# A fourth output buffer and a re-ordered step list in a fused chunk attention and leaky-ReLU MLP kernel

## Chip, cores and metric

The kernel runs on one core of a Trainium2 chip. The metric is the device time of one execution in microseconds (us), the median of several executions. TensorE appears in the profile as PE, its weight load as PEld, VectorE as DVE, ScalarE as ACT, GpSimd as POOL, and SyncE, which here only issues DMAs, as SP. The profile's times of day are counted from the start of the profiled span.

## What is computed

Attention is cut into chunks of 64 rows that attend only to themselves; its result is the input of a two-layer network with a leaky ReLU.

```python
B, H, S, D = 8, 8, 576, 64            # q, k, v: float32
scores = scale * matmul(q_c, k_c.T)   # per chunk of 64 rows
attn = exp(scores - max) / (sum + 1e-9)
x = (attn @ v_c) -> [4608, 512]       # heads side by side
h = x @ w_in                          # [512, 2048]
g = maximum(0.01 * h, h)
out = g @ w_out                       # [2048, 512], float32
```

## The kernel before

**Tiling.** The 4608 tokens are 36 attention units `u` of 128 tokens (two chunks, eight heads), and 19 network blocks `j`: two of 128 tokens and 17 of 256. Each block has one or two output tiles `(j, t)` of 128 tokens by 512 float32.

**The steps.** The whole program is a string, `ORDER` (L588 on); each word calls one small function, and the words are recorded one after the other. Every engine then runs its own instructions strictly in that order and waits by semaphores. The words that matter here, for a unit `u`:

- `g` loads q and k (DMAs issued by POOL, which also converts to 16 bits); `tdq`, `tdk` transpose them with DMAs issued by SP (early units use TensorE, `tq`, `tk`, and copies `q`, `k`); `cq` copies the transposed q into a padded tile `QZ`.
- `s` makes the scores on PE, `m`, `b`, `x` the maximum, subtraction and exponential, `z` the sum and its reciprocal, `n` the normalisation (a mark `'` behind the word puts it on POOL). `e` and `c` transpose it by PE and a copy, or `d` by a DMA of SP. `v` multiplies by v on PE, and `a` writes the result into `xT`.

For a block `j`: `M` and `G` are the first layer and its leaky ReLU in the plain form (blocks 0 to 4, 16 matmuls of 128 columns for each `M`). From block 5 on the first layer uses seven half-size products, `V` (eight matmuls of 128 columns), with input sums `xs`, and `ls`, `lf`, `la`, `lp` around them. The second layer of blocks 2 to 18 has seven products `R` (eight matmuls of 256 columns), with sums `sum` of the hidden tile and `comb`, which combines the products in PSUM banks into output tiles. `WS` and `W` make weight sums; `vl`, `L`, `Q`, `P` load v and the weights. `y` writes zeros. The mark `'` selects the other engine: ACT or DVE for copies, DVE or POOL for sums.

**Output tiles.** `st j.t` stores an output tile by a DMA that SP issues. Tiles of blocks 0 to 3 live in six buffers shared with another tile (`xkeep`); those of later blocks in three buffers (`osb`, L547). Which buffer of a pool a tile gets, and which of the eight PSUM banks, is read from a second string, `BANKS` (L60), one digit for each tile. The first `comb` that writes a tile has to wait until the store of the buffer's tile before has landed in DRAM. By the digits the three buffers hold, one after the other, tiles (4,1), (6,1), (7,0), (9,1) and on; (4,0), (5,1), (6,0), (8,0) and on; (5,0), (7,1), (8,1), (10,1) and on.

SP issues its DMAs one after the other: a store that stands behind a transposing DMA waits until that one's input is there. POOL likewise issues loads in turn with its own arithmetic.

Of the kernel before, what the change touches and what calls it, by code (L numbers as in the profile page):

```python
# [8 lines left out]
FP16 = mybir.dt.float16  # L9
# [7 lines left out]
def kernel(  # L17
# [32 lines left out]
    HELD = 4  # L50
# [5 lines left out]
    sbp = ctx.enter_context(tc.tile_pool(name="k_sb", bufs=1))  # L56
# [4 lines left out]
        "00011221230456070010314000500217016214111507112302062123352232304113201152167534233330222053401467100010334400"  # L61
        "13571420161745522311176641100130110257726203232163050000260305117211223311412623372234204331530060152344200551"
        "76234101020110541013101230220213272225140377333432006115001323040400114216105400241310267220022231311010114501"
        "20302011321141031325600202117010123032141013321723602700020334320410006101054120230105571104231101013212132223"
        "11173512271210632123416056144001202011322463002000602002110201273560300103311240120017011526411233342211712117"
        "30211760251213310314042330004123214003205600510031047223010526023052302110743112107213311343122116401101300371"
        "22420013213340503301105101017033102066146250311531210022127022413100002013471121702210311033430310711425330260"
        "02301257120457301061523222240310060004020113112353002142162111121340200111312701002032304353102213154002144303"
        "0106411732452411010211460174025322315100132310744021021127110405"
# [87 lines left out]
    warm = sbp.tile([128, 384], FP16, name="warm")  # L157
# [387 lines left out]
    def output(j, t):  # L545
        if (j, t) not in ob:
            tag, bufs = ("xkeep", 6) if j < HELD else ("osb", 3)  # L547
            ob[j, t] = sb([128, d_model], FP32, "ob", tag, bufs)
        return ob[j, t]
# [32 lines left out]
    def store(j, t, c=2):  # L582
# [146 lines left out]
```

## Time and profile before

| what | us |
|---|---|
| median of 3 timed runs (lowest, highest) | 277.01 (276.88, 281.54) |
| the profiled execution | 278.08 |
| its span, first to last instruction | 276.3 |
| PE busy | 264.6 |
| DVE, ACT, POOL busy | 236.6, 185.4, 142.9 |

The table of stretches that the prediction shows gives, for each piece of the span, how long each engine was busy; what is missing to the length of the stretch on PE is idle time of PE. A timeline row gives the start, the duration, the engine, the line and the operation with its tiles (out<-in), and in brackets the idle time of that engine before it and what ended it. Rows of equal instructions are merged (x8 are eight of them). In a chain-of-waits row "DMA out_dram<-ob" the first number is when SP issued the store, the second how long it was until it had landed.

### The profile page before, as it was taken

Reading aid. Unit: us, or ns where it says so; the run is one execution under the profiler, and the core shown is the slowest. Engines: PE = TensorE matmul, PEld = TensorE weight load, DVE = VectorE, ACT = ScalarE, POOL = GpSimd, SP = SyncE. Lnnn points to the kernel's source line nnn. Section 1 sums busy time; section 2 is a strip of 40 time slices with the busy share of each in tenths; the row PEclk is TensorE's granted clock in tenths of the full one; section 3 lists DMA queues with packets and bytes.
Section 4 is the critical chain, followed back from the end, with each engine's and each line's share of the span. In section 5 each row is a group of like instructions: output and inputs, shape, how many; then the busy total and the mean of one; then the engine's idle time right before and its main releaser. Section 6 shows DMA issues by size and latency. Waiting matters only on the chain.

```text
span 276.3 us, 9429 instructions
## 1 busy us (share of the span) xinstructions
PE 264.6 (96%) x3909; PEld 243.5 (88%) x3909; DVE 236.6 (86%) x487; ACT 185.4 (67%) x380; POOL 142.9 (52%) x174
## 2 busy tenths in 40 slices
PE   7889999999999998999899999999999999999994
PEld 4579967998999997889799999999999999999993
DVE  7785699988799997798799999998898996888873
ACT  4675735897859996679567784977878655536330
POOL 8858556887557949378549249646333122000000
PEclk9999999999999999999999999999999999999998
DMA  9999999999899999999999999999999231420323
GB/s 146 158 189 193 207 174 155 155 93 149 95 158 153 137 130 168 179 184 124 177 184 166 138 165 122 201 200 176 149 162 122 78 40 49 30 78 2 116 77 115
DMA packets 157611, 37.97 MB, mean 137 GB/s; under 512 B 148608, under 2 KB 153088, under 8 KB 157568
## 3 DMA queue, kind: packets, MB, share of 16 engines
q0 software_dynamic: 111392, 18.10, 98.8%
q1 hardware_dynamic: 45136, 19.02, 41.9%
q8 instruction: 30, 0.49, 0.8%
q10 hardware_dynamic: 1040, 0.26, 0.4%
q14 instruction: 13, 0.11, 0.1%
HBM read 36.70 MB, written 9.44 MB: 167 GB/s over the span
## 4 chain that ended last, share of the span: by engine, by line
PE 70%; DVE 12%; DMA 8%; ACT 5%; issue 2%; POOL 2%; SPq 0%; DVEq 0%; ACTq 0%; POOLq 0%
PE prX L525 16%; PE xbank L442 13%; PE prZ L525 9%; DMA out_dram<-ob 8%; PE hT L370 7%; PE xz L442 7%; PE prW L525 4%; PE seed L442 4%; PE oP L571 2%; PE xp L335 2%; PE Sp L277 2%; DVE SG L502 2%; DVE z L299 2%; DVE mx L284 2%; ACT gT L384 2%
## 5 line engine op out<-in xcount | busy, mean ns | idle before, releaser
L525 PEld LDWEIGHTS <-SG 128*128 128x128 f16 x544 | 51.1, 98 | 7.6 <-issue 2.1
L442 PEld LDWEIGHTS <-WS 128*128 128x128 f16 x896 | 54.6, 98 | 0.9
L309 POOL TENSOR_TENSOR en<-ex,z 128x512 f16<-128x512 f16 x30 | 31.5, 1056 | 40.1 <-DVE z L305 32.3
L442 PEld LDWEIGHTS <-w_inT 128*128 128x128 f16 x672 | 41.2, 98 | 1.6 <-issue 1.0
L525 PEld LDWEIGHTS <-gT 128*128 128x128 f16 x400 | 37.5, 98 | 3.9
L117 POOL DMA_DIRECT2D q_in<-in_q_dram x39 | 33.6, 867 | 14.1 <-DMA QT<-q_in 9.9
L117 POOL DMA_DIRECT2D k_in<-in_k_dram x39 | 32.8, 845 | 5.2 <-DMA VB<-in_v_dram 1.7
L525 PE MATMUL prX<-TW,SG 128*128 128x256 f16 x272 | 35.1, 273 | 0.0
L442 PE MATMUL xbank<-xs,WS 128*128 128x128 f16 x448 | 33.1, 219 | 0.0
L370 PE MATMUL hT<-xT,w_inT 128*128 128x128 f16 x512 | 31.7, 219 | 1.4 <-ACT ex L294 0.9
L370 PEld LDWEIGHTS <-w_inT 128*128 128x128 f16 x512 | 29.4, 98 | 1.9 <-issue 1.7
L299 DVE TENSOR_REDUCE z<-ex 128x8 f32<-128x512 f16 x36 | 24.0, 674 | 4.7 <-ACT ex L294 4.4
L200 ACT ACTIVATE keep<-prX 128x256 f32<-128x256 f32 x42 | 16.0, 382 | 16.8 <-PE prX L525 14.6
L284 DVE TENSOR_REDUCE mx<-Sp 128x8 f32<-128x512 f32 x36 | 24.3, 677 | 1.5 <-PE Sp L277 1.4
L502 DVE TENSOR_TENSOR SG<-gT 128x1024 f16<-128x1024 f16 x34 | 23.9, 707 | 2.0 <-ACT gT L384 1.7
L122 POOL DMA_DIRECT2D VB<-in_v_dram x24 | 23.3, 981 | 3.1 <-DMA w_outT<-in_moe_w_out_dram 3.1
L461 DVE TENSOR_TENSOR xz<-xbank,x 128x512 f32<-128x512 f32 x28 | 19.0, 690 | 3.3 <-PE xbank L442 1.6
L384 ACT ACTIVATE gT<-xz 128x512 f16<-128x512 f32 x28 | 16.6, 594 | 6.6 <-PE xz L442 6.5
L200 ACT ACTIVATE xT<-xp 128x512 f16<-128x512 f32 x26 | 15.4, 593 | 8.0 <-PE xp L335 7.8
L461 DVE TENSOR_TENSOR x<-xbank,x 128x512 f32<-128x512 f32 x28 | 19.0, 682 | 2.0 <-PE xbank L442 1.9
L384 ACT ACTIVATE gT<-seed 128x512 f16<-128x512 f32 x28 | 16.6, 598 | 6.1 <-PE seed L442 4.9
L384 ACT ACTIVATE gT<-xbank 128x512 f16<-128x512 f32 x28 | 16.1, 595 | 5.8 <-PE xbank L442 5.3
(97 smaller groups left out, 576.5 us busy)
## 6 DMA issues: line engine op xcount, KB each, us to landing
out_dram<-ob SPq DMA_DIRECT2D x35, 256.0 KB, 3.9
q_in<-in_q_dram POOLq DMA_DIRECT2D x31, 128.0 KB, 6.6
k_in<-in_k_dram POOLq DMA_DIRECT2D x31, 128.0 KB, 6.8
VB<-in_v_dram POOLq DMA_DIRECT2D x8, 288.0 KB, 7.9
VB<-in_v_dram POOLq DMA_DIRECT2D x16, 144.0 KB, 7.7
w_inT<-in_moe_w_in_dram POOLq DMA_DIRECT2D x8, 256.0 KB, 7.4
w_outT<-in_moe_w_out_dram POOLq DMA_DIRECT2D x4, 512.0 KB, 11.5
q_in<-in_q_dram POOLq DMA_DIRECT2D x8, 64.0 KB, 8.0
```

The lines of the kernel that those rows point to most:

```text
L117: nc.gpsimd.dma_start(out=to, in_=rows)
L122: nc.gpsimd.dma_start(out=VB[b % NVB][m * CH:(m + 1) * CH, h0:h1, :, m * CH:(m + 1) * CH].rearrange("p h c d -> p (h c) d"), in_=v[b, m * ...
L200: nc.scalar.activation(out=to, in_=of, func=AFT.Copy, bias=0.0, scale=1.0)
L284: nc.vector.tensor_reduce(out=MX[u], in_=SP[u], axis=AXL.X, op=ALU.max)
L299: nc.vector.tensor_reduce(out=Z[u, 0], in_=EX[u], axis=AXL.X, op=ALU.add)
L309: (nc.gpsimd if other else nc.vector).tensor_tensor(out=EN[u], in0=EX[u], in1=Z[u, 2].unsqueeze(2).to_broadcast((128, 8, CH)), op=ALU.mult)
L370: nc.tensor.matmul(out=hT[:, i, :], lhsT=w_inT[:, t, fc * 128:(fc + 1) * 128], rhs=xT[:, t, r0:r0 + tb], start=(i == 0 and t == 0), stop=( ...
L384: nc.scalar.activation(out=to, in_=of, func=AFT.Prelu, bias=0.0, scale=1.0, alpha=0.01)
L442: nc.tensor.matmul(out=to[:, i, :], lhsT=left[:, t, i * 128:(i + 1) * 128], rhs=right[:, t], start=(n in (1, 5) and t == 0 and i == 0), st ...
L461: nc.vector.tensor_tensor(out=to, in0=XB[j, s], in1=X5[j, s], op=ALU.add)
L502: (nc.gpsimd if other else nc.vector).tensor_tensor(out=SG[j, n], in0=x, in1=y, op=op)
L525: nc.tensor.matmul(out=to, lhsT=left[:, f, :], rhs=right[:, f, :], start=(f == 0 and (n in (1, 2, 5) or where == "Z3")), stop=(f == HF - 1 ...
```

## The change

Four edits. The pool `osb` has four buffers. The constant tile `warm`, which the first idle matmuls read, gets the memory of one of them (its tag). `BANKS` and `ORDER` are written anew from the 114th word on: the same 1551 words, in another order, and 134 of them with the mark `'` set or taken away.

```diff
@@ BANKS @@
-        "00011221230456070010314000500217016214111507112302062123352232304113201152167534233330222053401467100010334400"
+        "00011221230456070010314000500217016214111507112302062123352232304113201152167435233330204220335215416000300133"
...
-    warm = sbp.tile([128, 384], FP16, name="warm")
+    warm = sbp.tile([128, 384], FP16, name="warm", tag="osb4_0")
...
-            tag, bufs = ("xkeep", 6) if j < HELD else ("osb", 3)
+            tag, bufs = ("xkeep", 6) if j < HELD else ("osb", 4)
...
@@ ORDER @@
-        "P1 M0.2.0 z3.1 P2 z3.2 n3 G2.1.1 g7 M1.2.0 e3 M2.2.1 c3' v3 k4 a3 s4 M2.0.2 M2.1.2 M2.2.2 m4 b4 WS1.0 x4 z4.0 "
+        "P1 M0.2.0 z3.1 P2 z3.2 n3 M2.2.1 G0.2.0 G2.1.1 e3 M1.2.0 g6 k4 c3' G2.2.1 y5 s4 v3 M0.3.0 a3 G0.3.0 m4 M2.0.2 "
```

The four buffers now hold (4,0), (6,0), (8,1), (10,0) and on; (4,1), (6,1), (8,0), (10,1) and on; (5,0), (7,1), (9,0) and on; (5,1), (7,0), (9,1) and on. Of the words whose mark changes, the net effect is that six `a`, six `cq` and five `lp` go from DVE to ACT, seven `comb` from ACT to DVE, and five `xs` from DVE to POOL; `lf`, `ls`, `n`, `y` and `z` change by one each.

Three places where the order differs. First the queue of SP from the store of tile (4,0) on (`out_0_dram<-ob_1922`, and after the change `ob_1839`). Before it reads:

```order
L264 DMA_TRANSPOSE QT_2376<-q_in_1830 128x4x128
L326 DMA_TRANSPOSE et_2399<-en_2397 128x4x128
L585 DMA out_0_dram<-ob_1922 128x512
L258 DMA_TRANSPOSE KT_2411<-k_in_1832 128x4x128
L264 DMA_TRANSPOSE QT_2431<-q_in_2268 128x4x128
L326 DMA_TRANSPOSE et_2443<-en_2429 128x4x128
L258 DMA_TRANSPOSE KT_2476<-k_in_2270 128x4x128
L264 DMA_TRANSPOSE QT_2514<-q_in_2317 128x4x128
L258 DMA_TRANSPOSE KT_2642<-k_in_2319 128x4x128
L585 DMA out_0_dram<-ob_2422 128x512
```

The next store there, `ob_2422`, is tile (5,1), which uses the buffer of `ob_1922`. After the change the same stretch of SP is:

```order
L585 DMA out_0_dram<-ob_1839 128x512
L258 DMA_TRANSPOSE KT_2136<-k_in_1692 128x4x128
L585 DMA out_0_dram<-ob_2044 128x512
L585 DMA out_0_dram<-ob_1546 128x512
L264 DMA_TRANSPOSE QT_2242<-q_in_2006 128x4x128
L264 DMA_TRANSPOSE QT_2266<-q_in_2178 128x4x128
L326 DMA_TRANSPOSE et_2312<-en_2225 128x4x128
L258 DMA_TRANSPOSE KT_2314<-k_in_2008 128x4x128
L326 DMA_TRANSPOSE et_2358<-en_2346 128x4x128
L585 DMA out_0_dram<-ob_2397 128x512
```

Tiles (4,0) and (4,1), `ob_1839` and `ob_2044`, and the held tile (3,1), `ob_1546`, are stored ahead of the transposes, and (5,1), `ob_2397`, no longer shares a buffer with (4,0); `QT_2266` is `tdq20`, whose load `q_in_2178` is `g20`, and `et_2312` is `d14`.

Second, SP further on, around the store of tile (6,1) before (`ob_2775`):

```order
L585 DMA out_0_dram<-ob_1920 128x512
L264 DMA_TRANSPOSE QT_2709<-q_in_2401 128x4x128
L585 DMA out_0_dram<-ob_2373 128x512
L264 DMA_TRANSPOSE QT_2801<-q_in_2439 128x4x128
L326 DMA_TRANSPOSE et_2949<-en_2947 128x4x128
L585 DMA out_0_dram<-ob_2775 128x512
L258 DMA_TRANSPOSE KT_3027<-k_in_2441 128x4x128
```

After the change SP issues the stores of (5,0), `ob_2240`, and (6,1), `ob_2763`, in this stretch:

```order
L264 DMA_TRANSPOSE QT_2882<-q_in_2298 128x4x128
L258 DMA_TRANSPOSE KT_2926<-k_in_2255 128x4x128
L326 DMA_TRANSPOSE et_2928<-en_2679 128x4x128
L585 DMA out_0_dram<-ob_2240 128x512
L258 DMA_TRANSPOSE KT_2941<-k_in_2300 128x4x128
L264 DMA_TRANSPOSE QT_3076<-q_in_2534 128x4x128
L326 DMA_TRANSPOSE et_3128<-en_2943 128x4x128
L326 DMA_TRANSPOSE et_3139<-en_2964 128x4x128
L264 DMA_TRANSPOSE QT_3154<-q_in_2480 128x4x128
L585 DMA out_0_dram<-ob_2763 128x512
```

The store of (5,0), which was ahead of that of (6,1) by three entries, is now ahead by six, and each still stands behind transposes of normalised scores (`et<-en`).

Third, ACT at the first word that differs, where `xT` of unit 3 is written. Before:

```order
L200 ACTIVATE KT_650<-kp_520 128x512
L200 ACTIVATE xT_70<-xp_641 128x4x128
L294 ACTIVATE ex_719<-sh_715 128x512
L384 ACTIVATE gT_566<-hT_622 128x4x128
L384 ACTIVATE gT_458<-hT_571 128x4x128
```

After:

```order
L200 ACTIVATE KT_640<-kp_520 128x512
L384 ACTIVATE gT_566<-hT_595 128x4x128
L200 ACTIVATE xT_70<-xp_655 128x4x128
L384 ACTIVATE gT_458<-hT_664 128x4x128
L384 ACTIVATE gT_442<-hT_619 128x4x128
L294 ACTIVATE ex_744<-sh_742 128x512
```

Two leaky ReLUs (`G0.3.0` and `G1.2.0`, tiles `hT_664` and `hT_619`) now stand between the write of `xT` and the exponential of unit 4; on PE the 16 matmuls of `M0.3.0` stand between `v3` and `M2.0.2`, where before only the eight of `s4` did.

More of the change, by code (lines that the diff above doesn't have):

```diff
@@ L60 @@
     BANKS = (
-        "00011221230456070010314000500217016214111507112302062123352232304113201152167534233330222053401467100010334400"
[L62 to L69, printed above, removed]
+        "00011221230456070010314000500217016214111507112302062123352232304113201152167435233330204220335215416000300133"
+        "05714210131114622074412010011435673220555663300657700735121621342275233312370641141013315272332210000225123004"
+        "07055151026013306120334711123220154016422033022763421332653007305410112504234011560010322010022003324211212114"
+        "02506221527116304224705133112313051131306273121703373306250000060070101112133312261204414452071431011700222611"
+        "12343241623102032011016113532150531242040310212311516060077112000214331062230174302001324005012233102102345363"
+        "11240101310213241030033712103367110722000163126105303043112224400121120511031040074215622271201412521101243332"
+        "00311323370104710210220012037413003305204167002032141315061320060211173012163420102221101615122342332030133445"
+        "74012220010623230013700020104102026227351120216113104714604020412232171101133030223203510017301151207402204037"
+        "1103416073301231104153211261210142042122231402641500132020161210"
     )
```

169 rows, old and new, of the table ORDER are left out of this document.

## Prediction

> **What bounds the kernel now.** I read the stretches of the span first, then TensorE's idle times in the timeline, then what each of them waited for, then the prices of the instructions that change engines. The stretches (busy us of each engine in each window):
>
> ```profile
> span 276.3 us, 9429 instructions
> ...
> 0.00:30.00 30.00, 25.79 (x411) 20.21 (x412) 21.76 (x45) 17.55 (x29) 23.14 (x36) 1.00 1.57 174
> 30.00:68.00 38.00, 38.00 (x566) 33.39 (x564) 34.22 (x69) 27.45 (x56) 27.12 (x30) 1.00 2.00 152
> 68.00:104.00 36.00, 35.10 (x543) 33.42 (x541) 32.05 (x66) 30.63 (x66) 22.76 (x28) 1.00 1.79 138
> 104.00:136.00 32.00, 29.59 (x440) 27.70 (x438) 26.61 (x56) 24.02 (x51) 21.26 (x25) 1.00 1.95 163
> 136.00:174.00 38.00, 37.70 (x560) 35.77 (x560) 35.48 (x74) 26.31 (x56) 24.51 (x29) 1.00 1.79 159
> 174.00:272.60 98.60, 98.44 (x1400) 93.00 (x1399) 86.14 (x180) 59.43 (x127) 24.14 (x29) 1.00 0.74 104
> 272.60:276.30 3.70, 0.00 (x0) 0.00 (x0) 0.34 (x1) 0.00 (x0) 0.00 (x0) 0.76 0.37 128
> ```
>
> The first column after the comma is PE. It lacks 4.2 us in the first 30, 0.9 in the third row, 2.4 in the fourth, 0.3 and 0.2 in the next two, and the last 3.7 are the final store. From 174 us on PE is full; no order can shorten that part by more than 0.2. All matmuls stay in the program, so what can be won is PE's idle time, and only what lies behind the 114th word, at about 25 us. To see that PE is not only busy but fast, take rows that follow each other, and then its idle times:
>
> ```profile
> 97.98 1.04 PE L525 MATMUL prW<-w_outT,gT 128*128 128x256 f16 x8
> 98.85 0.61 PE L442 MATMUL xz<-xs,w_inT 128*128 128x128 f16 x8
> 99.30 0.61 PE L442 MATMUL xbank<-xs,WS 128*128 128x128 f16 x8
> ...
> 101.06 0.40 PE L335 MATMUL xp<-et,VB 128*128 128x64 f16 x8
> 101.30 0.40 PE L277 MATMUL Sp<-KT,QZ 128*128 128x64 f16 x8
> ...
> 28.58 0.61 PE L370 MATMUL hT<-xT,w_inT 128*128 128x128 f16 x8 [0.45 <-ACT xT L200]
> ...
> 69.31 0.89 PE L370 MATMUL hT<-xT,w_inT 128*128 128x128 f16 x13 [0.90 <-ACT ex L294]
> ...
> 105.62 0.60 PE L525 MATMUL prZ<-w_outT,SG 128*128 128x256 f16 x4 [0.84 <-DVE ob L563]
> ...
> 117.82 1.03 PE L525 MATMUL prZ<-TW,SG 128*128 128x256 f16 x8 [0.76 <-DVE ob L563]
> ...
> 135.21 0.61 PE L442 MATMUL xbank<-xT,w_inT 128*128 128x128 f16 x8 [0.61 <-DVE ob L563]
> ...
> 136.14 0.60 PE L525 MATMUL prZ<-w_outT,SG 128*128 128x256 f16 x4 [0.33 <-DVE ob L563]
> ...
> 174.04 0.61 PE L442 MATMUL seed<-xT,w_inT 128*128 128x128 f16 x8 [0.20 <-ACT seed L200]
> ```
>
> An `R` step takes 0.87 us from start to start, a `V` 0.45, a `v` or `s` 0.24; with these I count distances in the list. A group's own duration overlaps the next by 0.17 (97.98 + 1.04 against 98.85), so a gap costs its idle time and 0.17: 0.62, 1.07, 1.01, 0.93, 0.78, 0.50 and 0.37 us, 5.3 together. Four of the seven, 3.2 us, name a combine of DVE. That one waits for a store:
>
> ```profile
> 105.14 0.42 DVE L563 TENSOR_TENSOR ob<-prZ,keep 128x256 f32<-128x256 f32 x1 [1.86 <-DMA out_dram<-ob]
> ...
> 117.34 0.42 DVE L563 TENSOR_TENSOR ob<-prW,keep 128x256 f32<-128x256 f32 x1 [1.12 <-DMA out_dram<-ob]
> ...
> 134.73 0.42 DVE L563 TENSOR_TENSOR ob<-prW,keep 128x256 f32<-128x256 f32 x1 [1.81 <-DMA out_dram<-ob]
> ...
> 99.44 5.61 DMA out_dram<-ob
> 110.48 6.77 DMA out_dram<-ob
> 129.04 5.60 DMA out_dram<-ob
> ```
>
> These are `comb5.5`, `comb6.2` and `comb7.2`, the first writes of (5,1), (6,0) and (7,0). Each landing ends just ahead of the write: 99.44 + 5.61 = 105.05, 117.25, 134.64. DVE had come to the write 3.8, 5.7 and 3.9 us after the store was issued (its start less its idle time, less the issue), and the landing took longer.
>
> **The change, part by part.** *The fourth buffer and the places of the stores.* In the list before there are 0.9 (one `R`), 1.6 (three `V`, a `v`) and 5.1 us (three `R`, five `V`, an `s`) of PE work between the store and the first write into its buffer; the chip made 3.8, 5.7 and 3.9 of them, since SP ran ahead of the list by 2.9 and 4.1 us and once behind by 1.2. Now (5,0) and (5,1) meet empty buffers, and (6,0), (6,1) and (7,0) stand 19 us (9 `R`, 23 `V`, 5 short ones), 22 and 24 us behind the stores they wait for. No landing comes near that: all three waits go, -3.2 us.
>
> Two other distances become short: `st5.0` to `comb7.5`, 2.0 us (`R`, two `V`, `v`), and `st6.1` to `comb8.2`, 3.1 us. With SP ahead by the mean of the three, 1.9, they become 3.9 and 5.0; the mean of the three landings is 6.0, so DVE would wait 2.1 and 1.0 us, of which PE felt 3.2 of 4.8 before: 2.0 us. At the landing of the median store, 3.9 (row below), both cost nothing. At their worst (SP 1.2 behind, 6.8 of landing) DVE waits 6.0 and 4.9, and PE 7.3. I take +1.0, the middle of 0 and 2.0, as both ends have rows behind them.
>
> By the Trainium skill ("DMA: Bandwidth & Descriptors", section "Anatomy of one DMA — SWDGE (gpsimd) path") a DMA takes about 2.0 us plus its bytes at 436 GB/s; an estimate from this for a store of 256 KB is 2.6 us. By it none of the three waits could have been, and the two short distances are free, which makes the sum 1.0 lower; the rows of 5.6 to 6.8 us speak against it, though the section fits DMAs of the other path.
>
> *The place at 28.58.* Before, only `s4` stood between `v3` and the matmul that reads its `xT`, hence the 0.45 us. Now `M0.3.0` with 16 matmuls stands there (two `V`, 0.9), which covers the copy: -0.6. But ACT must then do two leaky ReLUs of 0.6 each behind `xT`, and `M2.1.2` needs the bank of the second: 1.8 us on ACT from `v3` on against 1.8 on PE with `M0.3.0` and `M2.0.2`, so a hop between the engines, some 0.4, shows. Net -0.2, between -0.6 and +0.2.
>
> *The gaps at 69.31 and 174.04*, 1.07 and 0.37. Their neighbourhood is re-ordered, so the old cause is gone, but no row says what comes late next. Between 0 and -1.4 I take -1.0, nearer to the gain, because DVE, on whose chain the first hung, gets lighter:
>
> ```profile
> L198 DVE CAST xT<-xp 128x512 f16<-128x512 f32 x10 | 6.8, 678 | 0.0
> L200 ACT ACTIVATE xT<-xp 128x512 f16<-128x512 f32 x26 | 15.4, 593 | 8.0 <-PE xp L335 7.8
> L198 DVE COPY QZ<-QT 64x512 f16<-64x512 f16 x21 | 6.6, 320 | 0.4
> L200 ACT ACTIVATE QZ<-QT 64x512 f16<-64x512 f16 x23 | 14.2, 622 | 0.2
> L382 DVE SCALAR_TENSOR_TENSOR gT<-x 128x512 f16<-128x512 f32 x7 | 4.8, 685 | 0.0
> L384 ACT ACTIVATE gT<-x 128x512 f16<-128x512 f32 x21 | 13.0, 629 | 2.5 <-DVE x L461 2.5
> L198 DVE COPY keep<-prX 128x256 f32<-128x256 f32 x9 | 3.8, 420 | 0.3
> L200 ACT ACTIVATE keep<-prX 128x256 f32<-128x256 f32 x42 | 16.0, 382 | 16.8 <-PE prX L525 14.6
> L418 POOL TENSOR_TENSOR xs<-xT 128x256 f16<-128x256 f16 x10 | 6.7, 671 | 8.2 <-DVE xT L198 4.2 <-ACT xT L200 4.0
> ```
>
> *The changed marks.* DVE: -6 x 0.678 - 6 x 0.320 - 5 x 0.685 + 7 x 0.420 = -6.5 us. ACT: 6 x 0.593 + 6 x 0.622 + 5 x 0.629 - 7 x 0.382 = +7.8. POOL: five sums at 0.671, +3.4. Single changes of the other words are below a us for each engine. I price all this at nothing: PE's row hides it, and ACT, with 24.0 busy of 32 us in the tight stretch, is the engine with room. If that cover goes, a copy on ACT at 0.6 us comes late for a product on PE, with the same order of price as the gaps above.
>
> *The tag on `warm`.* The idle matmuls that read it are over in the first 25 us, and the first `osb` tile is written after 80: 0. The last steps of the list end with the same product, combine and store, so the 3.7 us at the end stay.
>
> **The sum.** -3.2 + 1.0 - 0.2 - 1.0 = -3.4 us. The profiled execution took 278.08 (span 276.3 and 1.8 around it), so 274.7; the timed runs have their median at 277.01, 1.1 lower, so I carry the difference over: **273.6 us**.
>
> **The rivals.** *All gaps go.* For it speaks that the new list keeps a store and the next first write of its buffer over 4.7 us apart at every place but the two. It gives -3.2 - 1.4 - 0.6 = -5.2, 278.08 - 5.2 - 1.1 = 271.8 us. Against it speak the two short distances, and that DVE is still busy for some 230 of 276 us, so that a late input can find it occupied.
>
> *The waits only move.* The two short distances cost 2.0, the gaps of 1.4 return elsewhere, and the new hop shows: -3.2 + 2.0 + 0.2 and some such gap again of 1.0 is 0: 277.0 us.
>
> *SP is held up by a load, slower.* The rows that bear on it:
>
> ```profile
> POOL en L309 <- DVE z L305: 32.3, 13, 8.0
> POOL xs L418 <- DVE xs L418: 18.5, 4, 8.7
> ...
> out_dram<-ob SPq DMA_DIRECT2D x35, 256.0 KB, 3.9
> q_in<-in_q_dram POOLq DMA_DIRECT2D x31, 128.0 KB, 6.6
> ...
> et<-en SPq DMA_TRANSPOSE x27, 5.3
> ```
>
> `g20` now stands 2.7 us of PE work ahead of `tdq20` (an `R`, four `V`) where it had 6.2; its load lands 6.6 us after POOL issues it, so SP stands for 3.9 us, and all behind it too. `d14` is next, 1.6 us later in the list; it starts 2.3 us late, takes 1.2 to issue the transpose ahead and 5.3 to land, and `v14` needs it 11.0 us after its place. That leaves 2.2 us: from there on each us that POOL is late at `g20` is one on PE. POOL has waited up to 8.7 us at one instruction; then PE stands 6.5, which makes 273.6 + 6.5 = 280.1 us. It speaks against it that in the rows before POOL mostly waits for what PE has just made, so it is as far as the list.
>
> *POOL and DVE block each other.* If each of the five sums that POOL gains keeps DVE from starting for its 0.67 us at a place where PE waits, that is 3.4 us: 277.0. The Trainium skill has this rule ("SBUF — State Buffer", section "Who interferes with whom"): a DVE instruction with two inputs in SBUF and a GpSimd one that reads SBUF exclude each other for the whole instruction. The trace does not decide it: POOL's ten sums of the row above take 671 ns in the mean, and no row tells what DVE did meanwhile.
>
> **How the numbers follow.** The forecast holds with 0.55, all gaps gone 0.15, waits only moved 0.13, SP held up 0.11, blocking 0.06. What a measurement of this kernel can tell from no change is about 2%, 5.5 us: faster means below 271.5, slower above 282.5. Below 271.5 lies less than half of the best case and a little of the forecast's own spread: 0.09. Above 282.5 needs POOL to be over 11 us late at `g20`, or the worst of the short distances with nothing gained: 0.06. Within 2%: 0.85. The range goes from the best sum, 271.7, to just above the two rivals that end at 277.0, 277.6. The forecast's own is 272.4 to 275.6 (its short distances at 0 and at 2.0, and the other terms half a us to each side).
>
> **What would show it.** Right: no DVE row of L563 between 95 and 140 us that waits for `out_dram<-ob` over 1 us, PE lacking under 1.5 us between 104 and 136; DVE's busy time near 230, ACT's near 193. The short distances: waits at the first writes of (7,1) and (8,0). Early: a gap of 0.2 to 0.5 behind `M2.0.2` near 30 us in place of 0.45 ahead of it. SP held up: `tdq20` more than 4 us behind the DMA before it, and PE waiting at `v14`. The prediction is wrong if PE lacks more than 4 us between 30 and 272, or less than 0.5.

## The result and the profile after

| | median us (lowest, highest, executions) | ratio to before, 95% interval |
|---|---|---|
| before, timed beside the change | 278.09 (276.88, 281.54, 5) | |
| after | 275.17 (274.92, 275.53, 5) | 0.9895 [0.9852, 0.9937] |
| after, timed again beside 17 of before (278.15) | 275.37 (274.90, 277.18, 12) | 0.9924 [0.9891, 0.9958] |

The change makes the kernel faster by 0.8 to 1.1%, which is within the 2% that the prediction counted as no change. 273.6 us was predicted, with a range of 271.7 to 277.6. The ratios leave out executions that lie far above the fastest of their kernel, the medians do not; so a median and a ratio can differ below.

The profiled execution after took 275.17 us (span 273.0), the one before 278.08 (276.3). The stretches of the span after; behind the comma stand, as before, the busy us of PE, PEld, DVE, ACT and POOL:

```profile
30.00:68.00 38.00, 37.72 (x531) 32.86 (x531) 34.23 (x68) 25.51 (x53) 27.04 (x30) 1.00 1.95 156
68.00:104.00 36.00, 36.00 (x581) 34.57 (x579) 32.50 (x67) 31.60 (x67) 24.15 (x30) 1.00 1.84 153
104.00:136.00 32.00, 30.34 (x455) 28.59 (x453) 31.03 (x58) 23.67 (x51) 22.96 (x28) 1.00 1.78 160
136.00:174.00 38.00, 38.00 (x588) 36.30 (x585) 35.78 (x76) 30.32 (x65) 23.54 (x28) 1.00 1.99 158
174.00:269.30 95.30, 95.30 (x1352) 90.06 (x1349) 78.85 (x163) 61.48 (x127) 26.34 (x31) 1.00 0.72 102
```

PE is full from 68 to 104 us, where it lacked 0.9, and from 136 us to the end. Between 104 and 136 it still lacks 1.66 us, where it lacked 2.41, and DVE, which was busy for 26.6 of these 32 us, is now busy for 31.0. The line on the stores and the landing times of the same profile say that it isn't a store any more:

```profile
L585 SPq DMA_DIRECT2D out_dram<-ob x36: 332/524/1713, 59.7 to 270.1; - x36
...
who waited for it (us, times):
busy tenths in 40 slices 0000000000000000000000000000000000000000
DMA to landing us min/median/max: 1.8/3.9/7.5
```

The list of those who waited is empty: no instruction of any engine waits for a store. The landings themselves are what they were (the median store took 3.9 us before too). Three idle times of PE are left behind 25 us:

```profile
30.28 0.89 PE L370 MATMUL hT<-xT,w_inT 128*128 128x128 f16 x13 [0.28 <-ACT gT L384]
...
124.27 0.62 PE L442 MATMUL xbank<-xs,WS 128*128 128x128 f16 x8 [0.74 <-DVE xz L461]
...
126.25 0.61 PE L442 MATMUL xbank<-xs,WS 128*128 128x128 f16 x8 [0.91 <-DVE xz L461]
```

The first is the hop that was forecast behind `M2.0.2`. The two others, 0.91 and 1.08 us from start to start, are new. They wait for `la8.0.3` and `la8.1.3` on DVE. DVE's timeline there shows why these are late, and POOL's what ran beside:

```profile
120.22 0.37 DVE L563 TENSOR_TENSOR ob<-prZ,keep 128x256 f32<-128x256 f32 x1
120.51 3.10 DVE L502 TENSOR_TENSOR SG<-gT 128x1024 f16<-128x1024 f16 x1
123.53 0.69 DVE L461 TENSOR_TENSOR xz<-xbank,x 128x512 f32<-128x512 f32 x1
...
120.04 0.94 POOL L117 DMA_DIRECT2D k_in<-in_k_dram  x1
120.94 2.11 POOL L309 TENSOR_TENSOR en<-ex,z 128x512 f16<-128x512 f16 x2
```

The sum `sum7.3` takes 3.10 us. Sums of its form take 0.68 (the median of 34). Beside it POOL first writes the descriptors of the load `g25` and then makes two products, `n18'` and `n19'`.

So, from start to start: the store gaps are gone (3.2), as are those at 69 and 174 us (1.43) and a small one at 108 (0.18); the gap near 30 us shrank from 0.62 to 0.44; the two new ones cost 1.99. That is -3.0 of the 3.3 us by which the span is shorter; the rest lies in gaps under 0.2 us, which I did not follow. The time of the execution fell by 2.9 us only, since 2.1 us of it now lie around the span, where it was 1.8.

### The profile page after: what moved, and what is told of

Read it like the earlier page. It is cut to its first block, busy times and chain, and to the rows that moved or that the text cites. A ratio compares the mean times of both kernels' runs of the same rounds, so it can differ in the third digit from the quotient of the medians.

```text
span 273.0 us, 9442 instructions
## 1 busy us (share of the span) xinstructions
PE 264.5 (97%) x3909; PEld 243.6 (89%) x3909; DVE 235.3 (86%) x473; ACT 191.7 (70%) x390; POOL 145.4 (53%) x178
## 4 chain that ended last, share of the span: by engine, by line
PE 87%; DVE 8%; ACT 2%; issue 1%; DVEq 0%
PE prX L525 20%; PE xbank L442 17%; PE prZ L525 10%; PE hT L370 10%; PE xz L442 8%; PE prW L525 5%; PE seed L442 4%; PE Sp L277 3%; PE xp L335 3%; PE oP L571 3%; PE idle L194 1%; DVE z L299 1%; PE kp L222 1%; PE qp L222 1%; ACT QZ L200 1%
## 5 line engine op out<-in xcount | busy, mean ns | idle before, releaser
L309 POOL TENSOR_TENSOR en<-ex,z 128x512 f16<-128x512 f16 x29 | 30.6, 1060 | 52.5 <-DVE z L305 35.8
L502 DVE TENSOR_TENSOR SG<-gT 128x1024 f16<-128x1024 f16 x34 | 25.4, 753 | 3.8 <-ACT gT L384 3.8
L200 ACT ACTIVATE xT<-xp 128x512 f16<-128x512 f32 x32 | 18.7, 595 | 11.0 <-PE xp L335 10.9
L384 ACT ACTIVATE gT<-hT 128x512 f16<-128x512 f32 x32 | 18.0, 594 | 2.2 <-PE hT L370 2.0
L200 ACT ACTIVATE keep<-prX 128x256 f32<-128x256 f32 x32 | 12.1, 384 | 10.5 <-PE prX L525 10.5
```

What stands on the lines that cost most here:

```text
L200: nc.scalar.activation(out=to, in_=of, func=AFT.Copy, bias=0.0, scale=1.0)
L309: (nc.gpsimd if other else nc.vector).tensor_tensor(out=EN[u], in0=EX[u], in1=Z[u, 2].unsqueeze(2).to_broadcast((128, 8, CH)), op=ALU.mult)
L384: nc.scalar.activation(out=to, in_=of, func=AFT.Prelu, bias=0.0, scale=1.0, alpha=0.01)
L502: (nc.gpsimd if other else nc.vector).tensor_tensor(out=SG[j, n], in0=x, in1=y, op=op)
```

## The experiments

The list and the buffers were varied apart first, then the new gap was taken to pieces. Moving a word takes its digits in `BANKS` along, so no tile changes its bank or buffer by it.

**The fourth buffer in the old order.** Each new tile takes the buffer whose store was issued longest ago; `warm` gets the memory of one of them here too.

```diff
-            tag, bufs = ("xkeep", 6) if j < HELD else ("osb", 3)
+            tag, bufs = ("xkeep", 6) if j < HELD else ("osb", 4)
```

> The order and the marks of before, with a fourth buffer for output tiles and nothing else (each new tile takes the buffer whose store was issued longest ago). Theory (the store waits were the buffer's): the three waits of comb5.5, comb6.2 and comb7.2 on their stores go, PE's four gaps of 1.01, 0.93, 0.78 and 0.50 us behind them go, and the time is some 3.2 us under before, 274.9 against a median of 278.1 for before; the gaps at 69 and 174 us (1.07 and 0.37) stay. Rival (the new order made the gain, or the waits only move): the time falls by under 1 us.

Measured: ratio 0.9966 [0.9915, 1.0016], so no change that the runs can tell; median 279.46 of 12 executions, from 274.83 to 284.95. The profiled execution (276.16) has the waits gone, as the theory says: PE is busy for 31.90 of the 32 us between 104 and 136, where it lacked 2.41. But the time did not follow. In this profile ScalarE's copies into `x5`, whose tiles share the six buffers of `xkeep` with the held output tiles, wait for stores, and the first of them shows on PE:

```profile
89.54 0.60 ACT L200 ACTIVATE x<-xz 128x512 f32<-128x512 f32 x1 [1.33 <-DMA out_dram<-ob]
...
90.92 0.61 PE L442 MATMUL xbank<-xs,WS 128*128 128x128 f16 x8 [0.67 <-DVE xz L461]
...
147.04 0.60 ACT L200 ACTIVATE x<-xz 128x512 f32<-128x512 f32 x1 [1.74 <-DMA out_dram<-ob]
```

In the list of before `st0.0` stands 34 words ahead of `lf5.1`, and `st2.1` four words ahead of `lf10.0`. The first wait was there in the profile of before too (0.54 us on ACT, hidden); the second was not.

**The same kernel, profiled once more.**

> The order of before with the fourth buffer alone, once more for a second profile. Theory (times of the old order differ by how long its stores and transposes take to land): PE's gaps before 110 us differ from the first profile by about as much as the two times differ, the late gaps at 117, 134 and 136 us stay gone. Rival (the clock): no new gap, and the granted clock accounts for the difference.

279.97 us, 3.8 more than the first profile. The late gaps at 117, 134 and 136 us stay gone. The difference does not lie ahead of 110 us, as the theory had it, but in one wait at 150 us:

```profile
149.73 0.60 ACT L200 ACTIVATE x<-xz 128x512 f32<-128x512 f32 x1 [5.77 <-DMA out_dram<-ob]
...
151.48 1.01 PE L442 MATMUL seed<-xT,w_inT 128*128 128x128 f16 x8 [3.60 <-ACT seed L200]
152.29 1.06 PE L442 MATMUL xz<-xs,WS 128*128 128x128 f16 x8
153.14 1.06 PE L442 MATMUL xbank<-xs,WS 128*128 128x128 f16 x8
...
155.19 0.61 PE L442 MATMUL xbank<-xs,WS 128*128 128x128 f16 x8
```

It is `lf10.0` behind `st2.1`: 1.74 us of waiting in one execution, hidden, and 5.77 in the next, of which PE felt 3.77 from start to start. SP issued the store at 143.21 and at 143.97 us; it landed 3.8 and 5.7 us later, and ACT came to it 2.1 us after the issue in the one and at the issue in the other. The groups of eight matmuls behind it take 1.01 and 1.06 us where they take 0.61: the clock is lower there, as the last section tells. So the rival of the clock is half right: there is a new gap, and the clock adds to it. With the gap's 3.8 and some 1.6 for the clock this execution loses 5.4 us; the first one lost 0.7 more at 90 us and 1.0 more before 30 us, where its loads were late, which leaves about 3.7.

**The old order, four buffers, and those two stores earlier.**

```diff
-st1.0 R3.3 M4.2.2
+st1.0 st0.0 R3.3 M4.2.2
-st7.1 comb8.2 a18'
+st7.1 st2.1 comb8.2 a18'
```

> The order of before with the fourth buffer, and two stores of held tiles issued earlier: st0.0 right behind st1.0, and st2.1 right behind st7.1 (38 and 28 words). The run with the fourth buffer alone had ScalarE's copies into x5, which share six buffers with the held tiles, wait 1.33 and 1.74 us for these two stores, the first with a PE gap of 0.83 us at 90 us. Theory (the old order leaned on stores in this second pool of buffers too, and how long a store takes differs from run to run, which is why its times spread from 274.8 to 285): no wait on a store is left before the kernel's end, the gap at 90 us is gone, the median of its times is near 275.3 and the spread under 2 us, as for after. Rival (the spread comes from something else, as the granted clock or the loads at the start): the gap goes, the best time falls by up to 0.8 us, but the times still spread over 4 us and more.

Measured: ratio 0.9901 [0.9860, 0.9942], median 275.73 of 9, from 273.68 to 279.77. The median fell by 3.7 us against the fourth buffer alone, to 0.4 above what was expected; by the ratios the gain is 1.8 us, and their intervals just overlap. The spread did not go: it is 6.1 us, and 3.9 without the highest time. The profiled execution is that highest one. Its gap at 90 us is gone, but `lf10.0` still waits for `st2.1`, which SP issued at 142.1 us, only 1.2 and 1.9 us earlier than in the two profiles above. PE does not feel it here. PE's largest gap waits for another DMA of SP, a transpose:

```profile
146.67 0.60 ACT L200 ACTIVATE x<-xz 128x512 f32<-128x512 f32 x1 [1.40 <-DMA out_dram<-ob]
...
168.41 0.69 PE L335 MATMUL xp<-et,VB 128*128 128x64 f16 x16 [2.30 <-DMA et<-en]
```

The theory holds for `st0.0`. It does not hold for `st2.1`, whose wait is still there, nor for the spread: the two stores are not its only source. That these two stores were what held the old order up is made likely by the medians, but one profile does not show it.

**The new order on three buffers.** At three places four tiles are in use at once; three stores are issued earlier there.

```diff
-            tag, bufs = ("xkeep", 6) if j < HELD else ("osb", 4)
+            tag, bufs = ("xkeep", 6) if j < HELD else ("osb", 3)
...
-V8.1.5 comb6.4 sum7.2
+V8.1.5 comb6.4 st6.1 sum7.2
...
-sum13.4 comb12.5 V14.0.7
+sum13.4 comb12.5 st12.1 V14.0.7
...
-a33 comb14.2 ls17.0
+a33 comb14.2 st14.0 ls17.0
```

> The order of after on three buffers: as in it four tiles are in use at once in three places, three stores (6,1), (12,1) and (14,0) are issued earlier, right behind the last write of their tile; nothing else is moved. Its shortest distances from a store to the next tile in its buffer are 6 to 10 words, as in before. Theory (the fourth buffer is what removes the waits): waits on stores come back in the middle of the kernel at comb8.4 and comb12.2, and perhaps at comb10.2, at 1 us or more of lacking PE time each where DVE has no lead; the time is 1 to 3 us over after, 276.5 to 278. Rival (the new order makes the gain, the buffer nothing): within 0.5 us of after, 275.2.

Measured: ratio 1.0106 [1.0047, 1.0165], the fastest of 6 executions 279.70: slower than before by some 1%, and 4.8 us over the fastest of after, more than expected. Two waits on stores are back, at the two tiles forecast, (8,1) and (12,0) (on DVE `comb8.5`, which writes the other half of what `comb8.4` writes, and `comb12.2`), and PE waits behind them:

```profile
152.02 0.42 DVE L563 TENSOR_TENSOR ob<-prZ,keep 128x256 f32<-128x256 f32 x1 [3.02 <-DMA out_dram<-ob]
...
210.25 0.42 DVE L563 TENSOR_TENSOR ob<-prW,keep 128x256 f32<-128x256 f32 x1 [3.21 <-DMA out_dram<-ob]
...
152.49 1.03 PE L525 MATMUL prZ<-w_outT,SG 128*128 128x256 f16 x8 [1.86 <-DVE ob L563]
...
212.25 1.03 PE L525 MATMUL prX<-w_outT,gT 128*128 128x256 f16 x8 [1.14 <-DVE ob L563]
```

6.2 us of waiting on DVE cost PE 3.9 from start to start (2.03, 0.55 and 1.30), about the same two thirds as in the kernel before (3.2 of 4.8). Another 0.8 us is a wait of PE for a transposed tile at 127 us, which after does not have. The new order needs the fourth buffer; without it, it is worse than the old one.

**The sum behind the leaky ReLU's additions.**

```diff
-comb6.3 sum7.3 la8.0.3 z20.0 tdq21 lp8.1.2 V8.1.6 vl4.1 g25 R7.5 z20.1' comb7.6 lf8.1' la8.1.3 cq21.1'
+comb6.3 la8.0.3 z20.0 tdq21 lp8.1.2 V8.1.6 vl4.1 g25 R7.5 z20.1' comb7.6 lf8.1' la8.1.3 sum7.3 cq21.1'
```

> After with one word moved: sum7.3 on DVE stands behind la8.1.3 and no longer ahead of la8.0.3. Theory (DVE's two-input sum7.3 is held by GpSimd's two products en, 3.10 us for 0.68, and la8.0.3 and la8.1.3 behind it keep PE waiting 0.74 and 0.91 us): both PE gaps (1.08 and 0.91 by starts) go, since la8.0.3 then starts near 120.5; the sum itself runs after GpSimd's products are through, or is held for a part of them with nobody behind it that PE needs; 273.2 against 275.2 for after. Rival (PE would lose the same 2 us in the next place, since the DVE work only moves behind): 274.5 to 275.2.

Measured: 273.19 us (272.90 to 275.18, 6), ratio 0.9843 [0.9796, 0.9890]. That is 2.0 us under after, as the theory had it to a tenth; the rival's 274.5 is out. The sum comes when the products are through, and takes its usual time; PE has no gap behind 30.1 us:

```profile
120.53 0.70 DVE L461 TENSOR_TENSOR xz<-xbank,x 128x512 f32<-128x512 f32 x1 [0.18 <-PE xbank L442]
...
122.51 0.70 DVE L461 TENSOR_TENSOR xz<-xbank,x 128x512 f32<-128x512 f32 x1
123.12 0.68 DVE L502 TENSOR_TENSOR SG<-gT 128x1024 f16<-128x1024 f16 x1
```

**The products later, the sum at its place.** With the reciprocal that `n18'` needs behind `sum7.4`, both products leave.

```diff
-v17 z18.2 comb6.3 sum7.3
+v17 comb6.3 sum7.3
...
-sum7.4 V8.0.3 st5.0
+sum7.4 z18.2 V8.0.3 st5.0
```

> After with one word moved: the reciprocal z18.2 (0.20 us) on DVE stands behind sum7.4, so that GpSimd's products n18' and n19' start some 6 us later, while sum7.3 stands where it stood. Theory (the clash with GpSimd's products makes sum7.3 long): sum7.3 takes 0.7 us at its old place, both PE gaps go, 273.2 against 275.2 for after. Rival (something else holds sum7.3 there, for example GpSimd's descriptor writing for the load of k at 120.04 to 120.98 or the matmul it follows): sum7.3 stays near 3 us and so does the time, 275.2. A third way: the products now hold another DVE sum behind sum7.4, and the time stays between.

Measured: median 275.51 (273.55 to 278.15, 12), ratio 0.9897 [0.9861, 0.9933]; the profiled execution took 273.55. The sum takes 0.68 us, beside the same descriptor write, and both gaps are gone, so it is the products that hold it:

```profile
120.19 0.68 DVE L502 TENSOR_TENSOR SG<-gT 128x1024 f16<-128x1024 f16 x1
...
119.80 0.94 POOL L117 DMA_DIRECT2D k_in<-in_k_dram  x1
...
131.09 0.61 PE L442 MATMUL xz<-xs,WS 128*128 128x128 f16 x8 [0.49 <-POOL xs L418]
```

The three products that POOL now makes in a row (3.09 us from 125.48 on) push its sums `xs` back, and PE waits for one of them, 0.66 us at 131 from start to start. So a part of the gain is given back in another place; the third way was right in this, though not in the engine. In the profiled execution, the fastest of the 12, 1.6 us are left of the gain. By the ratio nothing is (0.9897, and 0.9895 for after). Why the median lies 2 us over the profiled execution is not shown.

**One product later.** Now the reciprocal of `n19'` alone is moved.

```diff
-vl4.0 V8.1.1 V8.0.5 xs8.2 xs8.4 sum7.1 z19.2 V8.1.5
+vl4.0 V8.1.1 V8.0.5 xs8.2 xs8.4 sum7.1 V8.1.5
...
-sum7.4 V8.0.3 st5.0
+sum7.4 z19.2 V8.0.3 st5.0
```

> After with one word moved: the reciprocal z19.2 on DVE stands behind sum7.4, so that of GpSimd's two products beside sum7.3 only n18' is left there (1.04 us). Theory (a two-input DVE sum is held until the whole GpSimd product is through, and for each of two that follow one another): sum7.3 takes 2.0 to 2.1 us where it took 3.10 with two products and 0.68 with none, the two PE gaps together are 0.9 to 1.0 us where they were 1.99, the time some 274.2. Rival (the sum is held once for as long as GpSimd needs from its loads on, whatever the number of products): 3.1 us as before; or it slips in ahead of the one product: 0.7 us.

A single execution: 276.63 us, not 274.2. The sum and the gap are as the theory says, the time isn't:

```profile
120.26 2.11 DVE L502 TENSOR_TENSOR SG<-gT 128x1024 f16<-128x1024 f16 x1
...
120.70 1.10 POOL L309 TENSOR_TENSOR en<-ex,z 128x512 f16<-128x512 f16 x1
...
161.74 2.17 DVE L502 TENSOR_TENSOR SG<-gT 128x1024 f16<-128x1024 f16 x1
...
165.70 1.05 PE L525 MATMUL prX<-TW,SG 128*128 128x256 f16 x8 [1.08 <-DVE SG L502]
```

3.10 us with two products, 2.11 with one, 0.68 with none; the gap that is left costs 0.99 us in place of 1.99. POOL is late from there on, and 41 us further another of its products meets another sum, which takes 2.17 us and costs PE 1.24. Two smaller gaps (0.45 and 0.90) come on the way.

**The load behind the products**, so that no descriptor write lies beside the sum.

```diff
-vl4.1 g25 R7.5
+vl4.1 R7.5
...
-n19' R7.7
+n19' g25 R7.7
```

> After with one word moved: the load g25 (two descriptor writes on GpSimd, 119.15 to 120.98 in the profile of after) stands behind the products n18' and n19', so that no descriptor write lies beside sum7.3. Theory (the products alone hold the sum): n18' starts near 120.4, as soon as its reciprocal is there, and the sum ends 0.56 us behind the second product, so it takes some 2.5 us, and the PE gaps together 1.3 to 1.5 us instead of 1.99. Rival (the descriptor write ahead is what keeps the sum waiting until the products take their turn): sum7.3 takes 0.7 us, no gaps, 273.2.

A single execution: 274.69 us; PE stands for 1.4 us at 16 us in it, where a load of v is late. Neither the theory nor the rival was right:

```profile
121.67 1.46 DVE L502 TENSOR_TENSOR SG<-gT 128x1024 f16<-128x1024 f16 x1
...
121.54 2.49 POOL L309 TENSOR_TENSOR en<-ex,z 128x512 f16<-128x512 f16 x2 [1.18 <-DMA out_dram<-ob]
```

(The releaser in the bracket is inferred, and here it is a store that POOL has no use for; the products' reciprocal on DVE ends just ahead of them, at 121.45.) The sum waits for the first product (1.04 us) and then goes ahead of the second, which takes 1.48 us of the 2.49 where a product takes 1.04. PE loses 0.37 us. So a product alone holds the sum, but it waited for both only where a descriptor write ran ahead of them. The two cases differ in more than the descriptor write (in after the sum starts 0.43 us ahead of the first product, here 0.13 us behind it), so what decides is not shown.

**Both gaps mended.** To the sum's new place comes `G1.2.0`, ahead of `G0.3.0`.

```diff
-a3 G0.3.0 m4 M2.0.2 G1.2.0 M2.1.2
+a3 G1.2.0 G0.3.0 m4 M2.0.2 M2.1.2
```

> After with sum7.3 behind la8.1.3 (that alone: 273.19) and with ScalarE's leaky ReLU G1.2.0 ahead of G0.3.0, so that PE's M2.1.2, which takes the bank that G1.2.0 reads, does not wait for both. Theory (the gap of 0.44 us at 29.5 us is this order on ScalarE): the gap goes, G0.3.0 has a bank that nobody needs at once, 272.75. Rival (PE waits for the token copy or the next bank instead): 273.2.

273.02 us (272.48 to 274.42, 6), ratio 0.9819 [0.9782, 0.9856]. The gap at 29.5 us is gone; the profiled execution has late loads at the start instead. Both kernels were timed once more on one chip:

> The changed kernel itself, on the same chip as the mended one. Theory (it leans on no store, but on one place where GpSimd's products meet a DVE sum): 275.2 again, within 0.5 us from run to run, 2.0 to 2.4 us over the mended kernel. Rival (its five runs so far were lucky, and it spreads like the old order with four buffers): times from 274.9 to 279 and over.

> The mended kernel (sum7.3 behind la8.1.3, G1.2.0 ahead of G0.3.0) beside the changed one. Theory: 272.7 to 273.0, 2.0 to 2.4 us under the changed kernel, of which 2.0 are the sum's place and 0.4 the place of the leaky ReLU. Rival (the place of the leaky ReLU is worth nothing, as its first median of 273.02 against 273.19 leaves open): 273.2.

After 275.37 (ratio 0.9924, interval above), mended 273.02 (272.69 to 274.65, 6; ratio 0.9831 [0.9778, 0.9883]). The mended kernel is 2.3 us faster than after and beats both. After's profile shows the same sum of 3.10 us again; its times reach up to 277.18, more than the half microsecond that I expected. Of the mended kernel PE has this:

```profile
0.00:30.00 30.00, 26.86 (x417) 21.25 (x418) 22.22 (x45) 19.17 (x32) 21.39 (x34) 1.00 1.58 172
30.00:267.10 237.10, 237.10 (x3496) 222.44 (x3493) 210.23 (x427) 172.38 (x359) 124.13 (x144) 1.00 1.47 136
```

From 30 us to the last product PE is busy without a break. What the place of `G1.2.0` is worth in time, 273.19 to 273.02, is less than the runs can tell; that its gap is gone is seen in the trace alone.

## Why the prediction was right, and where not

**The three store waits, -3.2: right.** No combine waits for a store after, and the old order with the fourth buffer has PE full in the same stretch, so the buffer is what removes them. But in time neither the buffer nor the order gained alone: in the old order two waits for stores of the other pool came up, one with a PE gap of 3.77 us, and the new order on three buffers was slower than before. The new order is not the only one that serves: the old order with four buffers and those two stores earlier has the ratio of after, 0.9901 against 0.9895, though its times spread more.

**The short distances, +1.0: wrong, they cost nothing.** The failed step is "With SP ahead by the mean of the three, 1.9, they become 3.9 and 5.0". SP issued the stores (5,0) and (6,1) far earlier; the rows are its issue and the write that might have waited:

```profile
116.99 0.53 SPq L585 DMA_DIRECT2D out_dram<-ob  x1
...
129.25 0.42 DVE L563 TENSOR_TENSOR ob<-prZ,keep 128x256 f32<-128x256 f32 x1
...
126.66 0.52 SPq L585 DMA_DIRECT2D out_dram<-ob  x1
...
142.24 0.41 DVE L563 TENSOR_TENSOR ob<-prW,keep 128x256 f32<-128x256 f32 x1
```

12.3 and 15.6 us lie between them, against 2.0 and 3.1 us of PE's work in the list: SP was 10 and 12 us ahead of it. The landings were not short: the two stores took 5.8 and 4.3 us, so with a distance of 3.9 the first would have been waited for. It is the lead alone that made them free. The lead of 1.9 was taken from the three places where a wait had shown, that is, from those where SP's lead was too short.

**The place at 28.58, -0.2: right in size and mechanism** (0.62 to 0.44), and the swap on ACT shows that it is the order of the two leaky ReLUs.

**The gaps at 69 and 174 us, -1.0: both are gone, -1.43.** Which word did it was not tried. The one at 174 also went with the buffer alone, in the old order.

**The marks, 0: right, as far as PE's gaps show.** None of them after waits for an instruction that changed its engine. DVE's busy time did not fall to 230 us but to 235.3: 2.4 of it are the sum's wait, which counts as busy. Of the rest a part is in the reckoning: the busy time counts overlapping instructions once, while the durations added up, without the sums of L502, fell by 6.0 us. The prediction's -6.5 also left out the five `xs` that DVE loses, some 1.5 us.

**The rival "SP is held up by a load": it did not come.** SP issued `tdq20` at 97.76 us, 1.3 us behind the transpose ahead of it, and its load `g20` had landed at 93.3.

**The rival "POOL and DVE block each other", given 0.06, came true at another place.** It was priced on the five sums that went to POOL; what blocked were two products that had been on POOL all along, and met a DVE sum by the new order. It cost 2.0 us from start to start. So PE lacked 1.66 us between 104 and 136, and the sign "under 1.5" failed. The Trainium skill ("SBUF — State Buffer", section "Who interferes with whom") says that a DVE instruction with two inputs in SBUF and a GpSimd one that reads SBUF exclude each other for the whole instruction. The traces agree: 0.68, 2.11 and 3.10 us with none, one and two products. The rule had been cited, and weighed by a count of instructions instead of by the places in the list where the two stand beside each other.

**The sum.** -3.2 + 0 - 0.2 - 1.6 + 2.0 is -3.0, where -3.4 was forecast: the 1.0 that did not have to be paid, the 0.6 more at the old gaps and the 2.0 not seen nearly cancel, which is luck. From 278.08 less 3.4 the forecast came to 274.7; the last step, "1.1 lower, so I carry the difference over", made it 273.6. With more executions the median of before is 277.8 to 278.2, not 277.01, so there was no such difference to carry. Without it the forecast would have missed by 0.5. The prediction's inner range does not follow from its terms: 273.6 less 1.0 and 0.5, and plus 1.0 and 0.5, is 272.1 to 275.1, not 272.4 to 275.6, and 275.17 lies at its upper end.

## What to carry to other kernels

When a store's wait is removed, list every other tile that shares a buffer with a store, in all pools, with its distance: the next one comes up, and since one store landed after 3.8 us in one execution and 5.7 in another, a wait that is hidden in one profile is not safe. When an order changes, look at each place where GpSimd's arithmetic stands beside a DVE instruction that reads two tiles from SBUF, and put what PE waits for ahead of that instruction. The lead of a queue over the list must be taken from the whole trace, not from the places where it ran out.

## What the runs showed of the hardware

**A held sum ends 0.56 us behind GpSimd's instruction.** In the 13 traces there are 22 sums of L502 that took over 0.7 us and ended 0.55 to 0.56 us after the end of an arithmetic instruction of GpSimd; a sum takes 0.68 us by itself. A DVE instruction that takes longer than its like by the rest of a neighbour's time is therefore waiting, though it counts as busy. What decides who goes first is open: with a descriptor write running, a sum that started 0.43 us ahead of two products came behind both; without one it went between them.

Not every long sum is held by arithmetic. 29 other sums in these traces took 0.79 to 1.42 us beside descriptor writes of GpSimd. The longest of them in after goes ahead of the product that follows the writes, so a descriptor write ahead of a product does not always put the sum behind it:

```profile
106.45 1.42 DVE L502 TENSOR_TENSOR SG<-SG,gT 128x1024 f16<-128x1024 f16 x1
...
106.61 0.89 POOL L117 DMA_DIRECT2D k_in<-in_k_dram  x1
107.50 1.27 POOL L309 TENSOR_TENSOR en<-ex,z 128x512 f16<-128x512 f16 x1
```

Most sums beside descriptor writes take their 0.68 us, as `sum7.3` did with the products later; what tells the two kinds apart is not shown.

**A long wait of PE costs clock behind it.** The granted clock (the last column but two) reads, in the second profile of the old order with four buffers:

```profile
147.90:151.20 3.30, 0.00 (x0) 0.00 (x0) 0.35 (x1) 1.44 (x3) 0.49 (x1) 1.00 2.78 123
...
151.40:154.60 3.20, 3.12 (x27) 2.96 (x27) 1.75 (x5) 2.20 (x6) 1.04 (x1) 0.50 1.84 198
154.60:160.00 5.40, 5.40 (x91) 5.18 (x89) 4.95 (x12) 3.81 (x9) 0.00 (x0) 1.00 0.96 130
```

And in that of the same with two stores earlier:

```profile
166.10:168.40 2.30, 0.01 (x1) 0.03 (x1) 0.79 (x2) 0.71 (x2) 2.30 (x3) 1.00 1.26 37
168.40:169.60 1.20, 1.19 (x26) 1.18 (x27) 0.69 (x1) 0.46 (x1) 1.20 (x2) 1.00 1.96 155
169.60:173.00 3.40, 3.40 (x33) 3.03 (x31) 1.93 (x4) 1.69 (x5) 3.40 (x5) 0.50 1.92 150
```

PE stood idle for 3.60 us in the one and 2.30 in the other (3.77 and 2.46 from start to start). Behind each idle time the clock is 0.50 for 3.2 us and more, in the second trace only after PE had worked for 1.2 us at the full clock. That is some 1.6 to 1.7 us of work lost each, an estimate from these rows (half of PE's busy time at 0.50). These are the two longest idle times of PE behind 25 us in the 13 traces, and the only ones that a lower clock follows before the last product. The next longest, 1.86 us in the new order on three buffers, is followed by a clock of 1.00 (152.5 to 156.0 us).

The Trainium skill ("TensorE: Matmul & The Clock Gate", section "What's actually happening") has such a gate, at half the clock after an idle window of about 3.4 us. The half and the length of the slow time agree, but 2.30 us of idle were enough here.
